# Three small reorderings in an attention-plus-MoE kernel: four products moved between transposes and x chunks, and an earlier place in the queue for a transposing DMA

## The chip, the cores and the metric

The kernel runs on one NeuronCore of a Trainium2 chip. The core has five engines that run their own instruction streams and wait for one another through semaphores: TensorE (PE, with its weight loads shown separately as PEld), VectorE (DVE), ScalarE (ACT), GpSimd (POOL) and SyncE (SP). SP computes nothing here; it issues DMAs, in order. The metric is the time of one execution on the device in microseconds (us), the median of several runs.

## What is computed

An "efficient attention" followed by a feed-forward layer with a snake activation. Eight batches of eight heads, 576 rows each, head dimension 64; the feed-forward part sees 4608 tokens of width 512 and a hidden width of 2048.

```python
q_s = softmax(q, axis=-1);  k_s = softmax(k, axis=2)
kv  = einsum('bhsd,bhse->bhde', k_s, v)
x   = einsum('bhsd,bhde->bhse', q_s, kv)          # then tokens x 512
h = x @ w_in
g = h + sin(alpha * h) ** 2 / alpha
out = g @ w_out
```

## The kernel before

**Tiles and stages.** The 4608 tokens are taken as nine tiles of 512 (`t` = 0 to 8). A tile needs the rows of one batch or of two neighbouring ones (576 rows against 512), so attention for batch `b` is worked off while tile `b - 1` is in its feed-forward part. The program order on every engine is written out by hand (`tc.manual_schedule()`), so an engine does exactly what the lines say, in their order; semaphores add only the waits.

**The feed-forward part of a tile.** `mm_h(t, ni)` makes one block of 128 hidden units: four matmuls of 512 columns from `win` and the transposed input `xT` into one PSUM bank (L254). ACT takes the sine (L260); the square is made by ACT (L262), POOL (L264) or DVE (L266); DVE combines both into `g` (L270), which also frees the bank. There are 16 blocks in a tile. The second products (`mm_o`, L274) multiply `g` with `wout`: 64 of them for a tile, 16 for each of four row blocks `j` of 128 rows. After a row block's sixteenth product, `evac_o` copies the bank into one of four buffers `o` (L286) and requests two stores on SP (L289). These products run one tile behind: a generator (`o_stream(t)`, or `o_quad` for tile 0) yields after each product, and `take(os, n)` takes the next `n`. So the kernel fills PE with products wherever something else would have to be waited for.

**Attention for a batch.** ACT takes the exponentials of q and k (L119), POOL or ACT and DVE cast v into `vb` (L138, L450). `norm_q` sums q's rows on DVE and divides (L146 to L153), giving `qn`. `kv_mm` makes kv on PE (L174, 72 small matmuls), `kv_norm` on DVE makes the block-diagonal `kbd` from it (L184, L187). x is `kbd` times the transposed q, `qT` (L223, L231), and a copy brings it to `xT` (L226, L468, L553, L558). `qT` comes about in two ways:

- Batches 0 and 1: by PE (`q_transpose_ii`, L203), into a PSUM bank and from there by a copy. For batch 1 this is `transpose_q1(ii)`, with a bank of pool `a` (two banks) and a copy on DVE (L458). `x_half(ii)`, the x matmuls of one half, takes its two banks from the same pool and is copied by ACT and DVE (L468).
- Batches 2 to 7: by a transposing DMA on SP (`q_transpose_dma`, L213). For batch 2 it is two DMAs, one for each half `ii`; chunks `c` = 0 and 1 of x need the first, chunks 2 and 3 the second. From batch 3 on it is one.

**Around the three places.** In tile 0's products (`o_quad`, L439 to L487) batch 1's attention is worked off: `x_half(0)`, `transpose_q1(1)`, two products, `kv_mm`, `kv_norm`, five products, `x_half(1)`. In tile 1's products (L534 to L560) batch 2's: 52 products are taken by L547, then come the four chunks of x with one product after each, and the last products after a further group of four x matmuls. In tiles 3 to 6 the loop at L592 runs over 16 blocks. At block `ni` = 4 it requests the transposing DMA for batch `t + 1` and, up to batch 7, the three loads of the batch after (`load_batch`, L98, 1.15 MB each). From block 9 on, `attn_back` (L569) uses the result, at every second block. After each block, `take` brings the number of products up to `want` (L602): 25, 27, 30, 32, 35 after blocks 0 to 4 in tile 3, and 23, 25, 28, 30, 33 in tiles 4 to 6.

SP's queue holds, in tile 3's first blocks: the stores of row block 0 of tile 2, the stores of its row block 1, the transposing DMA (which waits for POOL's `qn`), three loads.

Of the kernel before, what the change touches and what calls it, by code (L numbers as in the profile page):

```python
# [23 lines left out]
def kernel(  # L24
# [53 lines left out]
    def src_view(t, b):  # L78
        return t[b].rearrange("(i e) (p j) d -> (e p) i (j d)", e=2, j=J)
# [21 lines left out]
    def load_batch(b):  # L101
        load("q", q, b)
        load("k", k, b)
        load("v", v, b)
# [6 lines left out]
    def load_wout(n0, n1):  # L111
        nc.gpsimd.dma_start(out=wout[:, n0:n1, :], in_=wout_v[:, n0:n1, :])
# [13 lines left out]
    def exp_half(name, b, ii, j1=J):  # L126
        if ii == 0:
            A[name + "e", b] = att2.tile([128, J, 4 * D], BF16, name=name + "e")
        exp_to(A[name + "e", b][:, 0:j1], staged[name, b][:, :, 0:j1], (ii,))
# [60 lines left out]
    def q_tile(b):  # L190
        if ("qT", b) not in A:
            A["qT", b] = att2.tile([128, 2, J, 128], BF16, name="qT")
        return A["qT", b]
# [6 lines left out]
    def q_transpose_ii(b, ii, j0, j1, tp):  # L200

        for j in range(j0, j1):
            nc.tensor.transpose(tp[:, j - j0], A["qn", b][:, ii, j], identb)  # L203
# [36 lines left out]
    def bank(kind):  # L240

        if kind == "k":
            return ps_k.tile([128, 2, MF], F32, name="kvp", tag="a")[:, 0]
        pool = {"a": lambda: ps_h[0], "b": lambda: ps_h[1], "l": lambda: ps_l, "o": lambda: ps_o}[kind]()
        return pool.tile([128, MF], F32, name={"l": "lp", "o": "op"}.get(kind, "hp"), tag=kind)
# [140 lines left out]
    def h_slot(t, ni, sq, lag):  # L386
        hp = mm_h(t, ni, 2 if ni < (4, 1, 0)[min(t, 2)] else 0)
        lag.append((t, ni, hp, sine(t, ni, hp, sq)))

    def flush(lag, keep):  # L390
        while len(lag) > keep:
            combine(*lag.pop(0))

    def o_quad(t, accs, engs):

        R = range(4)
        by_m, by_n = [(n, m) for m in R for n in R], [(n, m) for n in R for m in R]
        orders = [by_m, by_n, by_n, by_n[:8] + [(n, m) for m in R for n in (2, 3)]]
        for c in R:
            for n, m in orders[c]:  # L400
                mm_o(t, m, 4 * c + n, accs[m])
                if c == 3 and n == 3:
                    evac_o(t, m, accs[m], engs[m])
                yield

    def take(it, n=1000):
        for _ in range(n):
            if next(it, 0) == 0:
                return
# [4 lines left out]
    with ES:  # L414
        def load_q1(ii):
            if ii == 0:
                staged["q", 1] = stage.tile([128, 4, J, D], F32, name="st_q", tag="st")
            st = staged["q", 1]
            DVE_CP(st[:, ii, 0, 0:1], zero)
            nc.sync.dma_start(out=st[:, ii::2, 0:8].rearrange("p i j d -> p i (j d)"),  # L420
                              in_=src_view(q, 1)[:, ii::2, 0:8 * D])

        def load_kv1():
            for n in "kv":
                staged[n, 1] = stage.tile([128, 4, J, D], F32, name=f"st_{n}", tag="st")
            for ii in range(2):
                for n, t in (("k", k), ("v", v)):
                    nc.sync.dma_start(out=staged[n, 1][:, ii::2].rearrange("p i j d -> p i (j d)"),
                                      in_=src_view(t, 1)[:, ii::2])

        late = {6: lambda: load_q1(0), 8: lambda: load_wout(8, 12), 10: lambda: load_wout(12, 14), 13: lambda: (load_q1(1), load_kv1())}
        for ni in range(nN):
            h_slot(0, ni, "DPPAPPAPPAAPPAPD"[ni], lag)
            flush(lag, 1)
            if ni in late:
                late[ni]()
        flush(lag, 0)

        accs = [bank(kind) for kind in "bbll"]  # L439
        os = o_quad(0, accs, [DVE_CP, ACT_CP, DVE_CP, DVE_CP])  # L440
        take(os, 46)
        for ii in range(2):
            exp_half("q", 1, ii, 8)
        norm_q(1, [GP, V], 8)
        GP_CP(held, staged["k", 1][:, 0, 0, 0:1])
        load_wout(14, 16)

        def cast_v1(ii, eng):
            vv = vb[1].rearrange("p j (i c) -> p i j c", i=4)
            eng(vv[:, 2 * ii:2 * ii + 2, :, 0:D], staged["v", 1][:, ii::2])  # L450

        exp_half("k", 1, 0)
        cast_v1(0, ACT_CP)
        exp_half("k", 1, 1)
        def transpose_q1(ii):
            tp = ps_h[0].tile([128, 8, 128], BF16, name="tp", tag="a")
            q_transpose_ii(1, ii, 0, 8, tp)
            DVE_CP(q_tile(1)[:, ii, 0:8], tp)  # L458

        transpose_q1(0)  # L460
        take(os, 4)

        def x_half(ii):
            xp = [bank("a") for _ in range(2)]
            for e in range(2):
                attn_chunk(1, 2 * ii + e, 0, 8, xp[e])
            for e in range(2):
                (ACT_CP, DVE_CP)[e](xT[:, 2 * ii + e, MF:2 * MF], xp[e])  # L468

        kv_mm(1, 0, ps_k, split=True)  # L470
        kv_norm(1, 0, 1)
        for b in range(2):
            DVE_CP(q8[:, 0, b, 0:1], zero)
            nc.sync.dma_start(out=q8[:, :, b], in_=src_view(q, b)[:, :, 8 * D:J * D])
        load_batch(2)
        cast_v1(1, DVE_CP)
        take(os, 4)
        x_half(0)
        transpose_q1(1)
        take(os, 2)  # L480
        kv_mm(1, 1, ps_k, split=True)
        kv_norm(1, 1, 2)
        take(os, 5)
        x_half(1)
        exp_to(A["qe", 1][:, J - 2:J], q8)
        nc.scalar.activation(zero, zero, AX.Sin)
        take(os)  # L487
        for ki in range(2):
            mm_h(1, 0, ki, ki + 1)
        norm_q8()  # L490
        load("q", q, 3)
        load("k", k, 3)
        load("v", v, 3)

        def late_q8(ni):
            if ni == 11:
                tp = ps_k.tile([128, 2, 2, 128], BF16, name="tp", tag="a")
                for b in range(2):
                    for ii in range(2):
                        nc.tensor.transpose(tp[:, ii, b], A["qe", 1][:, J - 2 + b, ii * 128:(ii + 1) * 128], identb)  # L500
                DVE_CP(A["qT", 1][:, :, J - 2:J], tp)
            elif ni == 15:
                xp = ps_k.tile([128, 4, 2, P], F32, name="xp", tag="a")
                for c in range(4):
                    ii, e = divmod(c, 2)
                    for b in range(2):
                        nc.tensor.matmul(xp[:, c, b], kbd[b][:, e, ii],
                                         A["qT", 1][:, ii, J - 2 + b, e * 64:(e + 1) * 64], start=True, stop=True)
                DVE_CP(xT[:, :, 16 * P:18 * P], xp.rearrange("p c b n -> p c (b n)"))

        for ni in range(nN):
            h_slot(1, ni, SQ[ni], lag)
            flush(lag, 1)
            late_q8(ni)
        cast_v(2, [GP_CP, GP_CP])
        flush(lag, 0)
# [17 lines left out]
    os = o_stream(1)  # L534
# [15 lines left out]
    for c in range(4):  # L550
        xp = bank("aabb"[c])[:, 0:6 * P]
        attn_chunk(2, c, 0, 6, xp)
        (ACT_CP, DVE_CP)[c % 2](xT[:, c, c0:c0 + 6 * P], xp)  # L553
        take(os, 1)
    xp = ps_a.tile([128, 2, 512], F32, name="xp", tag="a")[:, :, 0:6 * P]
    for c in range(4):
        attn_chunk(2, c, 6, 9, xp[:, c // 2, (c % 2) * 3 * P:(c % 2 + 1) * 3 * P])
# [22 lines left out]
    for t in range(3, nT):  # L580
        b = t + 1 if t + 1 < B else None
        os = o_stream(t - 1)
        done = 0
        if b is not None:

            exp_q(b)
            exp_k(b)
            cast_v(b, [GP_CP, GP_CP])
            norm_q(b, [GP])
            take(os, 8)  # L590
            done = 8
        for ni in range(nN):  # L592
            hp = mm_h(t, ni)
            if b is not None:
                if ni == 4:
                    q_transpose_dma(b)
                    if b + 1 < B:
                        load_batch(b + 1)
                attn_back(b, ni - 5)
            s = sine(t, ni, hp, "A")  # L600
            combine(t, ni, hp, s)
            want = 23 + 2 * (t == 3) + 21 * ni // 8 if b is not None else 4 * (ni + 1)  # L602
            take(os, min(64, want) - done)
            done = min(64, want)
        take(os)
# [36 lines left out]
```

## Time and profile before

| | |
|---|---|
| median of 3 runs | 284.15 us (284.1 to 284.52) |
| the profiled execution, whole time | 284.61 us |
| its span, first to last instruction | 282.8 us |
| granted TensorE clock | 1.00 throughout |
| busy time PE / ACT / DVE / POOL | 272.3 / 225.2 / 189.1 / 83.6 us |
| first product stretch (tile 0's, batch 1's attention) | about 28 to 45.6 us |
| second product stretch (tile 1's, batch 2's attention) | about 60 to 76 us |
| tiles 3 to 6 | from 93.5 us on, some 29.4 us each |

The rows of a timeline read: start, duration (us), engine, line, operation, output<-input, tile of the array, shape, count of merged instructions, and in brackets the engine's idle time before it with what ended it. A matmul's end is modelled, and the next one starts before it. "SPq" rows are the issue of a DMA, not its transfer; the chain of waits shows a transfer from its request to its landing. Releasers are inferred, and where several things were waited for the latest is named.

### The profile page before, as it was taken

Reading aid. Unit: us, or ns where it says so; the run is one execution under the profiler, and the core shown is the slowest. Engines: PE = TensorE matmul, PEld = TensorE weight load, DVE = VectorE, ACT = ScalarE, POOL = GpSimd, SP = SyncE. Lnnn points to the kernel's source line nnn. Section 1 sums busy time; section 2 is a strip of 40 time slices with the busy share of each in tenths; the row PEclk is TensorE's granted clock in tenths of the full one; section 3 lists DMA queues with packets and bytes.
Section 4 is the critical chain, followed back from the end, with each engine's and each line's share of the span. In section 5 each row is a group of like instructions: output and inputs, shape, how many; then the busy total and the mean of one; then the engine's idle time right before and its main releaser. Section 6 shows DMA issues by size and latency. Waiting matters only on the chain.

```text
span 282.8 us, 4841 instructions
## 1 busy us (share of the span) xinstructions
PE 272.3 (96%) x1857; PEld 128.0 (45%) x1857; DVE 189.1 (67%) x286; ACT 225.2 (80%) x320; POOL 83.6 (30%) x80
## 2 busy tenths in 40 slices
PE   2999999999999999999999999999999999999994
PEld 1444444444444444444544444444444444444443
DVE  3968778899977768756875677667775555555412
ACT  4889667999489998899989998999877777777400
POOL 2989411777666550035012500241000000000000
PEclk9999999999999999999999999999999999999999
DMA  6999989996599018931991099019011111111143
GB/s 256 306 195 234 300 278 320 361 352 226 125 233 387 6 37 198 386 116 35 263 398 42 14 271 404 23 24 160 2 37 37 37 39 37 37 37 43 44 103 74
DMA packets 39127, 45.80 MB, mean 162 GB/s; under 512 B 17072, under 2 KB 22464, under 8 KB 39104
## 3 DMA queue, kind: packets, MB, share of 16 engines
q1 hardware_dynamic: 33360, 40.57, 47.0%
q0 software_dynamic: 5552, 4.79, 10.1%
q8 instruction: 14, 0.23, 0.3%
q10 hardware_dynamic: 192, 0.14, 0.2%
q14 instruction: 9, 0.07, 0.1%
HBM read 36.71 MB, written 9.44 MB: 163 GB/s over the span
## 4 chain that ended last, share of the span: by engine, by line
PE 82%; DMA 6%; ACT 5%; issue 2%; DVE 2%; POOL 1%; SPq 1%
PE hp L254 35%; PE op L274 32%; PE lp L274 2%; PE hp L274 2%; PE lp L254 2%; DMA qT<-qn 2%; ACT s L260 2%; DMA win<-in_moe_w_in_dram 2%; PE xp L223 2%; DMA st_k<-in_k_dram 2%; PE kvp L174 1%; PE op L612 1%; PE op L254 1%; PE kvp L254 1%; DVE qs L151 1%
## 5 line engine op out<-in xcount | busy, mean ns | idle before, releaser
L270 DVE SCALAR_TENSOR_TENSOR g<-s,inva_sb,hp 128x512 bf16<-128x512 f32 x128 | 94.3, 746 | 58.6 <-ACT s L262 52.9
L254 PE MATMUL hp<-xT,win 128*128 128x512 bf16 x512 | 128.3, 379 | 0.7 <-DMA win<-in_moe_w_in_dram 0.7
L274 PE MATMUL op<-wout,g 128*128 128x512 bf16 x496 | 124.1, 379 | 0.0
L260 ACT ACTIVATE s<-hp,alpha_sb 128x512 f32<-128x512 f32 x128 | 86.2, 682 | 24.3 <-PE hp L254 23.9
L254 PEld LDWEIGHTS <-win 128*128 128x128 bf16 x576 | 56.0, 98 | 67.9 <-DMA win<-in_moe_w_in_dram 0.8
L274 PEld LDWEIGHTS <-g 128*128 128x128 bf16 x560 | 53.9, 98 | 61.1 <-issue 0.4
L262 ACT ACTIVATE s<-s 128x512 f32<-128x512 f32 x112 | 70.5, 630 | 3.5
L264 POOL TENSOR_TENSOR s<-s 128x512 f32<-128x512 f32 x29 | 30.3, 1061 | 21.6 <-ACT s L260 21.6
L153 POOL TENSOR_TENSOR qn<-qe,qs 128x1152 bf16<-128x1152 bf16 (+1 forms) x12 | 25.1, 2110 | 33.0 <-DVE qs L147 24.3
L286 DVE COPY o<-op 128x512 f32<-128x512 f32 (+2 forms) x33 | 22.1, 670 | 9.9 <-PE op L274 7.6
L138 POOL CAST vb<-st_v 128x1152 bf16<-128x1152 f32 x12 | 14.7, 1257 | 46.9 <-DMA st_v<-in_v_dram 32.9
L119 ACT ACTIVATE qe<-st_q 128x1152 bf16<-128x1152 f32 (+1 forms) x16 | 17.5, 1130 | 5.0 <-DMA st_q<-in_q_dram 4.8
L119 ACT ACTIVATE ke<-st_k 128x1152 bf16<-128x1152 f32 x16 | 17.9, 1151 | 1.5 <-DMA st_k<-in_k_dram 1.5
L146 DVE TENSOR_REDUCE qs<-qe 128x36 f32<-128x2304 bf16 x5 | 12.8, 2553 | 7.9 <-ACT qe L119 7.9
L226 DVE CAST xT<-xp 128x512 bf16<-128x512 f32 (+1 forms) x18 | 13.5, 751 | 0.1
L151 DVE TENSOR_REDUCE qs<-qe 128x16 f32<-128x1024 bf16 (+1 forms) x6 | 7.5, 1252 | 3.8 <-ACT qe L119 3.8
L119 ACT ACT_TABLE_LOAD x7 | 9.0, 1283 | 1.3 <-PEq L626 1.2
L274 PE MATMUL lp<-wout,g 128*128 128x512 bf16 x32 | 9.1, 380 | 0.0
L274 PE MATMUL hp<-wout,g 128*128 128x512 bf16 x32 | 8.9, 380 | 0.0
L223 PE MATMUL xp<-qT,kbd 128*128 128x256 bf16 (+1 forms) x40 | 8.2, 286 | 0.3 <-DMA qT<-qn 0.3
L174 PEld LDWEIGHTS <-ke 64*64 64x64 bf16 x576 | 5.7, 108 | 4.7 <-ACT vb L329 1.3
L187 DVE TENSOR_TENSOR kbd<-kvp,kvr 64x256 bf16<-64x256 f32 (+1 forms) x20 | 7.4, 368 | 0.5
(83 smaller groups left out, 135.6 us busy)
## 6 DMA issues: line engine op xcount, KB each, us to landing
out_dram<-o SPq DMA_DIRECT2D x70, 128.0 KB, 2.4
st_q<-in_q_dram SPq DMA_DIRECT2D x6, 1152.0 KB, 6.3
st_k<-in_k_dram SPq DMA_DIRECT2D x6, 1152.0 KB, 8.8
st_v<-in_v_dram SPq DMA_DIRECT2D x6, 1152.0 KB, 11.1
st_k<-in_k_dram SPq DMA_DIRECT2D x4, 576.0 KB, 6.7
st_q<-in_q_dram SPq DMA_DIRECT2D x4, 512.0 KB, 5.2
st_v<-in_v_dram SPq DMA_DIRECT2D x3, 576.0 KB, 7.6
wout<-in_moe_w_out_dram POOLq DMA_DIRECT2D x3, 512.0 KB, 9.6
```

The lines of the kernel that those rows point to most:

```text
L119: nc.scalar.activation(dst[:, :, ii * 128:(ii + 1) * 128].rearrange("p j (x d) -> p x j d", x=2), src[:, ii::2], AX.Exp)
L138: engs[ii](vv[:, 2 * ii:2 * ii + 2, :, 0:D], staged["v", b][:, ii::2])
L153: engs[ii % len(engs)].tensor_tensor(qn[:, ii, 0:j1].rearrange("p j (x d) -> p j x d", x=2), qe[:, ii], part.unsqueeze(3).to_broadcast([12 ...
L223: nc.tensor.matmul(xp[:, e, 0:n], kt[:, e, ii], qT[:, ii, j0:j1, e * 64:(e + 1) * 64], start=True, stop=True)
L226: eng(xT[:, 2 * ii:2 * ii + 2, c0:c0 + n], xp[:, :, 0:n])
L254: nc.tensor.matmul(hp, win[:, ki, ni * 128:(ni + 1) * 128], xT[:, ki, t * MF % NX:t * MF % NX + MF], start=(ki == 0), stop=(ki == 3))
L260: nc.scalar.activation(s, hp, AX.Sin, scale=alpha_sb[:, ni:ni + 1])
L262: nc.scalar.activation(s, s, AX.Square)
L264: nc.gpsimd.tensor_tensor(s, s, s, op=ALU.mult)
L270: nc.vector.scalar_tensor_tensor(G[t][:, ni], in0=s, scalar=inva_sb[:, ni:ni + 1], in1=hp, op0=ALU.mult, op1=ALU.add)
L274: nc.tensor.matmul(acc, G[t][:, ni, j * 128:(j + 1) * 128], wout[:, ni, :], start=(ni == 0), stop=(ni == nN - 1))
L286: eng(o[:, cols], acc)
```

## The change

Two products move from after batch 1's second transposes to before them. Two products move from the group after batch 2's x chunks to the place between its second and third chunk. And in tiles 3 to 6 the transposing DMA of q, with the three loads that follow it, is requested at block 3 and not at block 4.

```diff
         x_half(0)
+        take(os, 2)
         transpose_q1(1)
-        take(os, 2)
         kv_mm(1, 1, ps_k, split=True)
...
         (ACT_CP, DVE_CP)[c % 2](xT[:, c, c0:c0 + 6 * P], xp)
-        take(os, 1)
+        take(os, 3 if c == 1 else 1)
...
             if b is not None:
-                if ni == 4:
+                if ni == 3:
                     q_transpose_dma(b)
                     if b + 1 < B:
                         load_batch(b + 1)
```

In the order of instructions, PE has the two products of batch 1 ahead of all eight transposes, and the two products of batch 2 ahead of chunk 2. DVE, ACT and POOL keep their order. SP's order changes in tile 3 alone: the transposing DMA and the three loads stand ahead of the two stores of row block 1 there. In tiles 4 to 6 no store lies between the two positions.

## The prediction

> **What bounds the kernel now.** I read the page's busy times and chain first, then the busy time by stretch, then the order of instructions around the places that the diff touches.
>
> ```profile
> PE 272.3 (96%) x1857; PEld 128.0 (45%) x1857; DVE 189.1 (67%) x286; ACT 225.2 (80%) x320; POOL 83.6 (30%) x80
> PE 82%; DMA 6%; ACT 5%; issue 2%; DVE 2%; POOL 1%; SPq 1%
> ```
>
> TensorE is the bound: 272.3 of 282.8 us busy. The chain gives DMA 6%, of which qT<-qn is 2.4% or 6.8 us. This isn't time to be won: the chain was followed back through these transfers (2.86 and 3.98 us), but PE worked during most of both. What can be won is PE's own pauses, so I asked for the stretches (columns: stretch, its length, then each engine's busy time with instructions):
>
> ```profile
> 28.00:45.60 17.60, 17.14 (x159) 8.13 (x158) 13.55 (x26) 10.16 (x13) 4.62 (x5) 1.00 0.99 277
> 60.00:76.00 16.00, 15.93 (x150) 7.57 (x147) 15.27 (x22) 13.36 (x15) 10.79 (x8) 1.00 0.72 233
> 94.00:112.00 18.00, 17.70 (x152) 8.17 (x151) 12.60 (x18) 17.51 (x25) 6.52 (x5) 1.00 0.33 70
> 112.00:141.00 29.00, 29.00 (x208) 13.69 (x206) 20.18 (x29) 26.64 (x39) 6.48 (x4) 1.00 0.68 204
> ```
>
> Only the first three hold a pause (0.46, 0.07 and 0.30 us; from 112 to 264 us there is none). These figures are too small, for a matmul shows about 0.38 us while the next one starts earlier: eight of 512 columns start within 1.73 us (74.23 to 75.96), so one costs 0.216 us of PE's stream. A true pause is start to start, less 0.216 per matmul between.
>
> **Place A, batch 1's second transposes.** PE's, PEld's and DVE's instructions around them:
>
> ```profile
> 40.96 0.61 PE L231 MATMUL hp<-qT,kbd 128*128 128x512 bf16 x2
> 42.02 0.61 PE L203 MATMUL tp<-identb,qn 128*128 128x128 bf16 x8 [0.46 <-ACT xT L468]
> ```
> ```profile
> 44.38 0.21 PEld L231 LDWEIGHTS <-kbd 128*128 128x128 bf16 x2 [0.22 <-DVE kbd L187]
> ```
> ```profile
> 41.48 0.77 DVE L450 CAST vb<-st_v 128x1152 bf16<-128x1152 f32 x1 [0.33 <-DMA st_v<-in_v_dram]
> 42.28 0.69 DVE L468 CAST xT<-hp 128x512 bf16<-128x512 f32 x1
> 42.89 0.68 DVE L458 COPY qT<-tp 128x1024 bf16<-128x1024 bf16 x1
> 43.54 0.17 DVE L184 RECIPROCAL kvr<-kvp 128x2 f32<-128x2 f32 x1
> 43.74 0.59 DVE L187 TENSOR_TENSOR kbd<-kvp,kvr 64x128 bf16<-64x128 f32 x2
> ```
>
> The two x matmuls occupy PE to 40.96 + 0.43 = 41.39; the transposes start at 42.02, since their bank is freed by ACT's copy (L468, 41.39 to 41.97). Pause: 0.63 us. The change puts two products there, 0.43 us, to 41.82. The transposes still start at 42.02 and take 0.45 us, to 42.47. Then kv follows without the two products: 0.09 us to change over (42.90 to 42.99 before), 0.42 us of matmuls, to 42.98; five products, 1.08 us, to 44.06. There x_half(1) needs kbd, and kbd is made by DVE, whose five rows follow one another without a gap from 41.48 on, the first having waited for st_v. None of them starts sooner: L458 waits for DVE, not for PE's transposes (done by about 42.64, against 42.89). So the weights still load at 44.38 and the x matmuls still start at 44.50, which is where PE stands now too (44.28 + 0.216). The pause moves from 42.0 to 44.1: 0.20 us stay and 0.44 us are new. I cost A at **0**. Upper bound: should st_v land 0.33 us sooner than in this execution, DVE's chain starts that much sooner and A gains 0.33. A loss is excluded as long as the transposes start at 42.02: ACT's copy sets that, and the copy hangs on the x matmul ahead of it.
>
> **Place B, batch 2's x chunks.** PE's instructions, and the chain at that time:
>
> ```profile
> 72.70 0.38 PE L274 MATMUL op<-wout,g 128*128 128x512 bf16 x1
> 73.15 0.32 PE L231 MATMUL hp<-qT,kbd 128*128 128x384 bf16 x1
> ```
> ```profile
> 70.25 2.86 DMA qT<-qn
> 73.11 0.04 issue
> ```
>
> The third chunk waits for the second transposing DMA, which lands at 73.11. Pause: 73.15 - (72.70 + 0.216) = 0.23 us. Two more products ahead of it bring the chunk to 72.53 + 0.16 + 3 x 0.216 = 73.34, after the landing: the pause is filled, with 0.19 us to spare. The two products are missing from the eight after the chunks, so tile 2's first block starts at 75.96 - 0.23 = 75.73. What it waits for: bank a (ACT's copy of chunk 0, done at 73.0) and chunks 1 to 3 in xT, needed by its second to fourth matmul. The last copy on DVE ends near 75.7 and the fourth matmul starts at 76.38: 0.7 us of cover. So B gains **0.23**. Bounds 0 and 0.23 (nothing more is idle there).
>
> In the Trainium skill, "TensorE: Matmul & The Clock Gate", section "Back-to-back issue gap", matmuls of 512 columns in a real stream are given about 131 ns each. By that figure two products would fill only 0.26 us of A's pause, and B's would just be covered; the 0.216 us of this trace decides.
>
> Is B's gain kept until place C? After 76 us ACT waits for PE at 77.02 and 83.05 (3.04 and 0.64 us idle), so the sines follow PE; POOL's first square (78.49) is held by norm_q and doesn't move, but its block's bank is wanted only at 81.97, against a combine done at 80.3. Tightest is tile 3's block 4: it starts at 102.13, its bank is free at 102.0. That combine follows ACT, which runs without idle time from 83.05, where it followed PE; both move by 0.23.
>
> **Place C, tile 3's q.** PE, SP's queue, and POOL:
>
> ```profile
> 110.31 1.03 PE L254 MATMUL hp<-xT,win 128*128 128x512 bf16 x4
> 111.63 0.39 PE L223 MATMUL xp<-qT,kbd 128*128 128x256 bf16 x2 [0.30 <-DMA qT<-qn]
> ```
> ```profile
> 102.68 4.82 SPq L289 DMA_DIRECT2D out_dram<-o  x4
> 107.60 1.87 SPq L213 DMA_TRANSPOSE qT<-qn  x1
> ```
> ```profile
> 99.64 4.21 POOL L153 TENSOR_TENSOR qn<-qe,qs 128x1152 bf16<-128x1152 bf16 x2 [3.33 <-issue]
> ```
>
> Pause: 111.63 - (110.31 + 4 x 0.216) = 0.46 us; tile 4 goes from the same block to its x matmuls in 0.86 us (139.80 to 140.66), with none. The request is queued on SP behind the two stores of tile 2's second row block, whose copy (DVE, 105.69) comes late, while qn was ready at 99.64 + 4.21 = 103.85. At block 3 the request stands ahead of these stores: block 3's share of products is the one that ends at number 32 and evacuates. The first two stores are issued by 103.8, so the request goes out at about 103.87 and lands, at the same 3.98 us, by 107.9; PE wants it at 111.17, less B's 0.23. Cover: 3.1 us. C gains **0.46**, bounds 0 and 0.46.
>
> What else moves with it: the three loads of batch 5 go out 3.7 us sooner, and the two stores behind them, at about 107.5 instead of 106.39. The stores now lie behind 3.4 MB: stores that do took up to 10.4 us to land. Their buffer (one of four) is written again four copies later, near 136 us (136.27). Nobody waits.
>
> In tiles 4 to 6 no store lies between the two positions (30 products are done by block 3's end, 33 by block 4's), SP's order is the same, and its request starts as soon as POOL ends: 133.32 against 129.08 + 4.22 = 133.30, and the like at 162.41 and 191.83. Block 3 or 4 means nothing to a queue that waits for POOL: **0**.
>
> **Sum.** 0 + 0.23 + 0.46 = 0.69 us. The profiled execution took 284.61 (a span of 282.8, and 1.8 around it), 0.46 above the median of the three shown, 284.15. It should come to 283.92, and the median to 284.15 - 0.69 = **283.46**.
>
> **Rivals.**
> 1. *The time comes back as another wait (283.7 to 284.15).* A pause on PE that is filled helps only if no other wait is as late. For: A is such a case, and ACT is busy 17.51 of 18 us between 94 and 112. Against: after C ACT waits for PE again (0.64 us at 113.36, 0.38 at 119.68), and the banks have the margins named above. Losing C alone gives 284.15 - 0.23 = 283.92, losing B alone 283.69, losing both 284.15. In this rival stands too that half of the change (A, tiles 4 to 6) does nothing, which my sum holds already.
> 2. *A pays as well (283.13).* 283.46 - 0.33, if st_v lands sooner than in this execution. Against: it is a fixed queue of loads from the same start.
> 3. *Slower: GpSimd's cast of v beside DVE (285.2).* The loads of batch 5 land 3.7 us sooner, so POOL's cast of v (L138, 122.38, which waited for them) runs at about 118.5, beside DVE's copies and combines of tile 3's blocks 13 to 15. For: DVE's product at 67.54, beside POOL, took 1.97 us for 1152 columns where 1024 took 1.23, 0.59 more than in proportion; three operations stretched so cost 1.8 us: 283.46 + 1.8 = 285.2. Against: beside that same cast, DVE's combine at 122.46 took 0.74 and its copy at 123.11 0.68, as elsewhere, and DVE waits 0.98 us for ACT at 121.06. It decides once 0.69 + 0.57 = 1.26 us of it reach PE.
>
> The Trainium skill, "GPSIMD Engine Reference", section "Specifications", says that GpSimd shares its path to SBUF with VectorE, with contention for some DVE instructions, those with two SBUF inputs among them; a combine reads one input from PSUM, so it would leave the third rival without a price.
>
> **How the numbers follow.** A measurement of this kernel tells about 0.2%, 0.57 us, from no change. Forecast 0.61, rival 1 0.23, rival 2 0.07, rival 3 0.09. The forecast's own range is 283.3 to 283.7 (the three runs before spread over 0.42). Faster by over 0.2% means below 283.58: 0.85 of the forecast and all of rival 2, 0.59; the rest of the forecast and rival 1 are within 0.2%, 0.32; slower 0.09. The range goes from rival 2 (283.1) to nearly all of rival 1 (284.1), and leaves out rival 3 and the edges.
>
> **What would show it.** A: the transposes still at 42.02, a new pause of some 0.4 us ahead of the x matmuls at 44.5 and tile 1's first block still at 45.58. B: no wait for qT between the second and third chunk, tile 2's first block at 75.7. C: SP's request at about 103.6, ahead of two stores, and no wait for qT at L223; all later PE rows 0.69 us sooner. I am wrong if the x matmuls of A start before 44.4, if a wait for ACT or a bank appears on PE in tiles 2 to 4, or if the last matmul isn't some 0.7 us sooner.

## The result, and the profile after

| | before | after |
|---|---|---|
| median, 17 runs each, one beside the other | 284.52 us (lowest 283.97) | 283.37 us (lowest 282.98) |
| ratio of the undisturbed runs, 95% interval | | 0.9957 (0.9944 to 0.9970) |
| the profiled execution: whole, span | 284.61, 282.8 us | 283.31, 281.5 us |

The change makes the kernel 0.43% faster (0.30 to 0.56%), some 1.2 us (0.85 to 1.6). The time of 283.37 lies close to the 283.46 that was forecast, but the gain is larger than the sum of 0.69 us: beside the new kernel, the old one measured 284.52 and not 284.15. So the closeness is in part luck: the starting value was 0.37 us too low and the gain 0.46 us too small, and the two nearly cancel. The larger gain is what has to be explained. One run of the kernel before, 288.73 us, 1.7% above its fastest, counts as disturbed.

The page of the kernel after, busy times and chain:

```profile
PE 270.0 (96%) x1828; PEld 128.3 (46%) x1857; DVE 188.8 (67%) x286; ACT 225.3 (80%) x320; POOL 83.5 (30%) x80
PE 85%; DMA 7%; POOL 2%; DVE 2%; issue 1%; ACT 1%; SPq 1%; ACTq 0%
```
PE's count is 29 matmuls lower than before while its weight loads are as many: records are missing, so the lower busy time tells nothing. The time has to be read from start to start. These are the same landmarks in each trace: the first product of the first stretch, the x matmuls of `x_half(0)` and `x_half(1)`, tile 1's first block, and so on to the first matmul of the last row block (L612).

| from one landmark to the next, us | before | after | difference |
|---|---|---|---|
| start of the span to the first product | 28.23 | 27.80 | -0.43 |
| first product to `x_half(0)` | 12.73 | 12.86 | +0.13 |
| `x_half(0)` to `x_half(1)`: place A | 3.54 | 3.34 | -0.20 |
| to tile 1's first block | 1.08 | 1.09 | +0.01 |
| to the first x chunk of batch 2 | 26.58 | 26.52 | -0.06 |
| to tile 2's first block: place B | 3.80 | 3.57 | -0.23 |
| to tile 3's block 9 | 34.35 | 34.35 | 0 |
| block 9 to tile 3's x matmuls: place C | 1.32 | 0.86 | -0.46 |
| from there to L612 | 163.96 | 163.95 | -0.01 |

The rows add up to -1.25 us, from 275.59 to 274.34 at L612 (the table's figures are rounded). B and C gave what was forecast. A gave 0.20, and 0.05 behind it (0.01 lost and 0.06 gained), where nothing was forecast. What stands ahead of `x_half(0)`, the first 41 us, which the change doesn't touch, gave 0.30 in this pair of executions.

Place A after the change, PE, then PE's weight loads, then DVE:

```profile
41.10 0.59 PE L274 MATMUL lp<-wout,g 128*128 128x512 bf16 x2
41.72 0.61 PE L203 MATMUL tp<-identb,qn 128*128 128x128 bf16 x8
42.26 0.48 PE L174 MATMUL kvp<-vb,ke 64*64 64x65 bf16 x36
...
43.54 0.38 PE L274 MATMUL lp<-wout,g 128*128 128x512 bf16 x1
44.00 0.60 PE L231 MATMUL hp<-qT,kbd 128*128 128x512 bf16 x2
```
```profile
43.99 0.11 PEld L231 LDWEIGHTS <-kbd 128*128 128x128 bf16 x2 [0.57 <-DVE kbd L187]
```
```profile
41.16 0.76 DVE L450 CAST vb<-st_v 128x1152 bf16<-128x1152 f32 x1 [0.31 <-DMA st_v<-in_v_dram]
41.95 0.69 DVE L468 CAST xT<-hp 128x512 bf16<-128x512 f32 x1
42.56 0.68 DVE L458 COPY qT<-tp 128x1024 bf16<-128x1024 bf16 x1
43.16 0.16 DVE L184 RECIPROCAL kvr<-kvp 128x2 f32<-128x2 f32 x1
43.35 0.59 DVE L187 TENSOR_TENSOR kbd<-kvp,kvr 64x128 bf16<-64x128 f32 x2
```

The two products now fill most of the old pause (41.10 to 41.53, transposes at 41.72), and a new pause stands ahead of the x matmuls: 44.00 - (43.54 + 0.216) = 0.24 us, with the weight load waiting for kbd. That is the picture of the forecast. What differs is the end: the x matmul starts at 44.00, 0.01 us after its weights begin to load, not 0.12 after. The load costs PE's stream next to nothing here: tile 1's first block follows the x matmul by 1.09 us, against 1.08 before.

Place C after the change, SP's queue and PE:

```profile
101.91 1.12 SPq L289 DMA_DIRECT2D out_dram<-o  x2
103.13 1.95 SPq L213 DMA_TRANSPOSE qT<-qn  x1
...
106.96 1.33 SPq L289 DMA_DIRECT2D out_dram<-o  x2
```
```profile
109.53 1.02 PE L254 MATMUL hp<-xT,win 128*128 128x512 bf16 x4
110.39 0.38 PE L223 MATMUL xp<-qT,kbd 128*128 128x256 bf16 x2
```

The request stands ahead of the two stores, 4.5 us sooner in the span (107.60 before), and the x matmuls follow block 9 after its four matmuls (4 x 0.216 = 0.86), without a wait.

### The profile page after: what moved, and what is told of

Read it like the earlier page. It is cut to its first block, busy times and chain, and to the rows that moved or that the text cites. A ratio compares the mean times of both kernels' runs of the same rounds, so it can differ in the third digit from the quotient of the medians.

```text
span 281.5 us, 4812 instructions
## 1 busy us (share of the span) xinstructions
PE 270.0 (96%) x1828; PEld 128.3 (46%) x1857; DVE 188.8 (67%) x286; ACT 225.3 (80%) x320; POOL 83.5 (30%) x80
## 4 chain that ended last, share of the span: by engine, by line
PE 85%; DMA 7%; POOL 2%; DVE 2%; issue 1%; ACT 1%; SPq 1%; ACTq 0%
PE op L274 38%; PE hp L254 37%; DMA st_v<-in_v_dram 4%; PE xp L223 2%; DMA win<-in_moe_w_in_dram 2%; DMA st_k<-in_k_dram 2%; PE kvp L174 2%; PE lp L254 2%; POOL s L264 1%; PE op L612 1%; PE op L254 1%; ACT s L260 1%; PE kvp L254 1%; POOL st_v L299 1%; DVE g L270 1%
## 5 line engine op out<-in xcount | busy, mean ns | idle before, releaser
L274 PE MATMUL op<-wout,g 128*128 128x512 bf16 x477 | 121.6, 379 | 1.4 <-issue 0.6
```

Of the source, the lines that this page charges most:

```text
L274: nc.tensor.matmul(acc, G[t][:, ni, j * 128:(j + 1) * 128], wout[:, ni, :], start=(ni == 0), stop=(ni == nN - 1))
```

## The experiments

Four kernels came first, each timed beside the kernel before on one chip (12 runs each, 35 of before, whose median was 284.43 us).

**A alone.**

```diff
         x_half(0)
+        take(os, 2)
         transpose_q1(1)
-        take(os, 2)
```

> Only the two products ahead of batch 1's second transposes (place A). The prediction's theory: A is worth 0, within 0.1 us of before; in the trace the transposes wait for ACT's copy as before, and a pause of about 0.4 us stands ahead of the x matmuls that need kbd. Rival theory, that A is where the 0.3 to 0.5 us come from by which the whole change gained more than the 0.69 us of the sum: 0.3 to 0.5 us faster, and tile 1's first block starts that much sooner after the stretch's first product. Third theory, that the surplus comes from the first 28 us and not from the change: no difference here.

Measured: 284.08 us, ratio 0.9984 (0.9961 to 1.0007). The comparison alone doesn't settle it; the trace does. `x_half(0)` to `x_half(1)` is 3.23 us against 3.54: 0.31 us. The prediction's 0 falls, and the rival's size (0.3 to 0.5) is met at this place. By the landmark that the expectation names, from the stretch's first product to tile 1's first block, it is only 0.21 us (17.14 against 17.35), for the part ahead of `x_half(0)`, which the edit doesn't touch, took 0.10 longer in this execution.

**B alone.**

```diff
-        take(os, 1)
+        take(os, 3 if c == 1 else 1)
```

> Only the two products between batch 2's second and third x chunk (place B). The prediction's theory: 0.23 us faster, no wait for qT ahead of the third chunk, tile 2's first block 0.23 us sooner after the first chunk; place C's wait for qT stays at 0.46. Rival: the pause comes back as a wait for a copy or for ACT in tile 2, then 0. The third theory adds nothing to the difference.

Measured: 284.38 us, ratio 0.9993 (0.9974 to 1.0011). In its trace the third chunk doesn't wait, and tile 2's first block comes 3.57 us after the first chunk, as forecast. But so it does in two kernels that don't have B at all, see below.

**C alone.**

```diff
-                if ni == 4:
+                if ni == 3:
                     q_transpose_dma(b)
```

> Only the earlier request of the transposing DMA in tiles 3 to 6 (place C). The prediction's theory: 0.46 us faster, all of it in tile 3, whose x matmuls follow block 9 without a pause. Rival: the earlier loads or the later stores cost part of it, then 0 to 0.3 us. If C alone gives 0.8 us or more, the surplus over the sum lies here, against the prediction's bound.

Measured: 284.06 us, ratio 0.9977 (0.9959 to 0.9995), 0.37 us by the medians. In the trace block 9 is followed by the x matmuls after 0.87 us; the pause of 0.46 is gone and nothing takes its place: from the x matmuls to L612 it is 163.95 us, as before.

**C in tiles 4 to 6 alone.**

```diff
-                if ni == 4:
+                if ni == (4 if t == 3 else 3):
                     q_transpose_dma(b)
```

> The earlier request in tiles 4 to 6 alone, and in tile 3 at block 4 as before. Every engine's order of instructions is that of before, so the prediction's theory says 0.00 us, and the measured difference shows what the comparison itself can tell. The theory that the surplus lies in how a newly built program happens to start says that this one, too, is some 0.3 to 0.5 us away from before.

Measured: 284.30 us, ratio 0.9992 (0.9973 to 1.0011). As forecast, nothing; with each engine's order unchanged this kernel is another execution of the kernel before. As such it showed that B's pause isn't always there. PE's instructions at the chunks, and SP's first transposing DMA, in this kernel:

```profile
72.09 0.33 PE L231 MATMUL hp<-qT,kbd 128*128 128x384 bf16 x1
72.25 0.38 PE L274 MATMUL op<-wout,g 128*128 128x512 bf16 x1
72.47 0.33 PE L231 MATMUL hp<-qT,kbd 128*128 128x384 bf16 x1
```
```profile
67.87 1.38 SPq L213 DMA_TRANSPOSE qT<-qn  x1
```

The third chunk follows the product after 72.47 - 72.25 = 0.22 us: no pause. SP took 1.38 us to issue the first of the two DMAs, against 1.82 us in the profile of before, and the second is issued only after it.

Then four kernels on a second chip (12 runs each, 35 of before, median 284.39): whether A pays in the whole, and what limits it.

**B and C without A** (the diffs above), and **the whole change again.**

> The change without its first part: B and C, A as before. The prediction's theory (A is worth 0): 0.69 us faster than before, and the same as the whole change run beside it. The theory formed after the first four runs (A is worth 0.2 to 0.35 us, B 0.05 to 0.23 by execution, C 0.46): about 0.55 us faster than before, and 0.2 to 0.35 us slower than the whole change.

> The whole change again, for the comparison with the other three on the same chip. The prediction's theory: 0.69 us faster than before. The later theory: 0.8 to 1.0 us faster.

Measured: B and C 283.72 us, 0.9976 (0.9955 to 0.9997); the whole 283.49 us, 0.9968 (0.9949 to 0.9988). By the medians 0.67 and 0.90 us: A is worth 0.23 in this comparison, whose intervals overlap. By the traces `x_half(0)` to `x_half(1)` takes 3.53 us without A and 3.21 with it, 0.32.

**The whole change with the copy of the transposes on ACT, and the kernel before with that copy alone.** The edit, in both:

```diff
             q_transpose_ii(1, ii, 0, 8, tp)
-            DVE_CP(q_tile(1)[:, ii, 0:8], tp)
+            (DVE_CP, ACT_CP)[ii](q_tile(1)[:, ii, 0:8], tp)
```

> The whole change, and the copy of batch 1's second transposes (L458) on ACT, which is idle for 2 us there, and not on DVE. The later theory says that after the change the x matmuls of x_half(1) wait for kbd at the end of a chain on DVE (cast of v, copy of x, copy of the transposes, kv_norm), so that taking 0.6 us out of that chain removes the pause ahead of them: kbd some 0.4 us sooner, the x matmuls 0.2 to 0.4 us sooner against the first product of the stretch, the kernel 0.2 to 0.4 us faster than the whole change. Rival, that PE's own products set the start of the x matmuls: no difference to the whole change.

> The kernel before with that copy on ACT alone. If the pause of A is on PE as the prediction says (five products end just when kbd is ready), a sooner kbd finds PE still at its products, and the kernel is within 0.1 us of before: the two edits pay only together. If DVE's chain were the limit in the kernel before as well, this alone would give 0.2 to 0.4 us.

Measured: the whole with it 283.30 us, 0.9969 (0.9946 to 0.9993); before with it 284.52 us, 1.001 (0.9984 to 1.0035). Both profiles are of executions that began late (the first product at 29.49 and 29.35 us, PE waiting 0.79 and 0.87 us for batch 0's cast of v), so only the distances behind it are used. With the whole change `x_half(0)` to `x_half(1)` is 3.10 us: exactly the two products less than 3.53, no pause ahead of `x_half(1)` left. In the kernel before it is 3.53 as ever. That kernel doesn't test what it was meant to, for kbd came no sooner: DVE's L184 waits 0.88 us there for kv on PE, and kbd is ready 3.37 us after `x_half(0)`, as in the profile of before. What set the x matmuls is read from the starts instead: in every execution without A's edit, and in those with the copy on ACT, they start 0.216 us after the last product, without a pause. So the limits are these: before the change, PE's own five products; after it, DVE's chain to kbd; with the copy on ACT, PE again.

Last, **the whole change and its ACT variant side by side** on a third chip (6 runs each, 11 of before, median 284.67), and **the kernel before in two more executions.**

> The whole change beside its variant with the copy of the transposes on ACT, on one chip. The later theory (A 0.25 to 0.38, B 0 to 0.24 by execution, C 0.46): 0.8 to 1.0 us faster than before. The prediction's sum: 0.69.

> The whole change with the copy of batch 1's second transposes on ACT. If the pause ahead of x_half(1) that the change leaves (0.1 to 0.2 us in the traces) is all that goes, it is 0.1 to 0.2 us faster than the whole change, and the x matmuls of x_half(1) follow those of x_half(0) by 3.10 us, against 3.2 to 3.3 in the whole change. Rival: the longer copy on ACT delays something in tile 1, then it is the same as the whole change.

> The kernel before, one more execution, to see which of its pauses are there each time. The prediction took all from one execution: 0.63 us ahead of the second transposes, 0.23 ahead of the third chunk, 0.46 at tile 3's qT. The later theory: the first and the last are there every time, the one ahead of the third chunk only where the first transposing DMA takes 1.8 us to issue and not 1.4; and the stretch's first product starts anywhere from 27.8 to 28.3 us.

> The kernel before once more, another execution, with what was expected of the first look: the pause ahead of the third chunk goes with the issue time of the first transposing DMA, the other two are there each time.

Measured: the whole 283.23 us, 0.9959 (0.9945 to 0.9973); the variant 283.30 us, 0.9956 (0.9941 to 0.9972). The variant's trace shows what was expected, PE's weights and DVE:

```profile
44.49 0.21 PEld L231 LDWEIGHTS <-kbd 128*128 128x128 bf16 x2 [0.22 <-DVE kbd L187]
```
```profile
43.64 0.17 DVE L184 RECIPROCAL kvr<-kvp 128x2 f32<-128x2 f32 x1 [0.55 <-PE kvp L174]
```

DVE now waits 0.55 us for kv, the copy being gone from its queue, and the x matmuls come 3.10 us after those of `x_half(0)`, at 44.60, where PE's products end. Against 3.2 to 3.3 in the whole change that is 0.1 to 0.2 us, and 0.05 of it is given back in tile 1. On the clock the variant came out 0.19 us ahead in one comparison and 0.07 behind in the other: no difference is shown, and there is no version that is shown to beat the change.

The two executions of before took 284.71 and 284.78 us, first product at 28.13 and 28.40. Their pauses at A and C were there (3.54 and 3.53 us; 0.48 and 0.49 us). At B one had none, and the other this, PE's chunks and SP's first transposing DMA:

```profile
72.59 0.38 PE L274 MATMUL op<-wout,g 128*128 128x512 bf16 x1
73.25 0.32 PE L231 MATMUL hp<-qT,kbd 128*128 128x384 bf16 x1 [0.28 <-DMA qT<-qn]
```
```profile
68.22 2.04 SPq L213 DMA_TRANSPOSE qT<-qn  x1
```

The pause is 73.25 - (72.59 + 0.216) = 0.44 us, twice that of the first profile. Over the seven executions that don't have B's edit:

| issue of the first transposing DMA, us | 1.38 | 1.39 | 1.57 | 1.62 | 1.80 | 1.82 | 2.04 |
|---|---|---|---|---|---|---|---|
| pause ahead of the third chunk, us | 0 | 0 | 0 | 0.02 | 0.20 | 0.23 | 0.44 |

(The kernels: C in tiles 4 to 6, A alone, the second of these two executions, before with the ACT copy, C alone, the profile of before, the first of the two. The 1.39 is worked out: the pair took 2.78 and the second of it 1.29, with 0.10 between.) Above 1.6 us the pause is the issue time less 1.6. Why SP needs longer for the same DMA in one execution than in another wasn't tried and stays open.

## Why the prediction was right, and where it wasn't

**What bounds the kernel, and where time could come from: right.** PE's pauses, read start to start, were the whole gain that the traces show behind `x_half(0)`. The rest of PE's stream kept its length in every trace: from tile 2's first block to tile 3's block 9 34.34 to 34.35 us, from tile 3's x matmuls to L612 163.94 to 163.96 us. Rival 1 (the time comes back as another wait) is thereby out, but for A, where the forecast itself had the new pause, and where it is smaller than forecast.

**C: right in place and size.** 0.46 us forecast; the pause was 0.46 to 0.54 in the seven traces without C's edit in tile 3, and 0.00 or 0.01 in the seven with it. The request came at 103.13; forecast was 103.6 less the 0.43 by which this execution began sooner. The stores that it passed went out at 106.96, and no one waited. Tiles 4 to 6: nothing, as forecast.

**B: right for the execution it was read from, wrong as a bound.** "Bounds 0 and 0.23 (nothing more is idle there)" took one execution for all. The pause was 0 to 0.44 us in seven, 0.13 on average; the two products, 0.43 us, cover nearly all of it. In the profile after, the gain was 0.23.

**A: the step that failed.** The prediction put it so: "So the weights still load at 44.38 and the x matmuls still start at 44.50, which is where PE stands now too", and therefore A at 0. The traces show 0.20, 0.31, 0.32 and 0.26 us in the four kernels with A (3.34, 3.23, 3.21 and 3.28 us against 3.53 or 3.54), and a further 0.05 in tile 1 up to the x matmuls of late q rows (14.11 or 14.12 us against 14.16 or 14.17; why this part shortens wasn't looked into). The prediction had also named a sign of being wrong, x matmuls of A that start before 44.4. They start at 44.00, or at 44.30 if `x_half(0)` is laid where it was before (40.96), so by its own sign this part is wrong; and the pause it expected ahead of them, some 0.4 us, is 0.24. The picture was right, the pause did move to the x matmuls, but the chain was over-long in two places:

- The weight load was counted in series, 0.12 us between 44.38 and 44.50. Before the change, the x matmul began at 44.50 because PE's products ended there; the load had merely happened in the meantime. Where PE stands idle, the matmul begins with the load: 43.99 and 44.00 after the change. The profile of before shows the same at C, where the load (the row below) and the matmul both start at 111.63. The Trainium skill says so too ("TensorE: Matmul & The Clock Gate", section "Architectural detail: the array is 16× 32×32, not 1× 128×128": a matmul can begin before its weights are completely loaded); I didn't hold it against this step.

```profile
111.63 0.11 PEld L223 LDWEIGHTS <-kbd 128*128 128x128 bf16 x2 [0.79 <-DMA qT<-qn]
```

- "None of them starts sooner" was true of that execution alone, and there not quite. In the six other executions without A's edit that have the copy on DVE (the kernel before twice more, B alone, C alone, C in tiles 4 to 6, B and C), DVE's L184 waits 0.17 or 0.18 us for kv on PE, which stands behind the two products that the change moves ahead; the row below is of the second further execution of before. In the first profile st_v had come 0.33 us late, and that wait was hidden but for 0.05 (L458 to L184 took 0.65 us before, 0.60 after).

```profile
43.94 0.17 DVE L184 RECIPROCAL kvr<-kvp 128x2 f32<-128x2 f32 x1 [0.17 <-PE kvp L174]
```

In the pair of profiles the load starts 3.42 us after `x_half(0)` before and 3.33 after (0.09), and the x matmul 0.12 and 0.01 us after the load (0.11): together 0.20. In the other kernels with A it is more, where DVE's cast of v (L450), which waits for st_v, starts sooner. Times from `x_half(0)`:

| kernel with A | change | A alone | the whole again | the whole, third chip |
|---|---|---|---|---|
| cast of v starts, us | 0.50 | 0.38 | 0.37 | 0.44 |
| x matmuls of `x_half(1)`, us | 3.34 | 3.23 | 3.21 | 3.28 |

The second row is the first plus 2.84 or 2.85 each time: DVE's chain from the cast on sets it. Without A's edit the cast starts anywhere from 0.17 to 0.52 us, and the x matmuls stay at 3.53 or 3.54. So rival 2 was right that A pays and that st_v decides how much, but the size of its bound, 0.33, was met by luck: it was to take st_v 0.33 us sooner, and 0.15 was enough. Nor is it a bound: by the same relation a cast that starts 0.26 us or less after `x_half(0)`, as in three of the executions without the edit, would leave PE's products as the limit, 3.10 us and a gain of 0.43. That is an estimate; no run with the copy on DVE shows it. And "a fixed queue of loads from the same start" doesn't land at a fixed time.

**The sum.** With the means of the traces A is 0.27 + 0.05, B 0.13, C 0.49: 0.94 us, inside the intervals of the first comparison (0.85 to 1.6) and the third (0.8 to 1.6), both of which leave out the forecast's 0.69, and near the second's medians (0.90), whose interval holds both. The first and third comparisons gave 1.15 and 1.44 us by the medians. What lies above 0.94 isn't settled. In eleven of the fourteen profiles the first product starts between 27.79 and 28.40, with and without the change (the kernel before at 28.13 to 28.40, in the order of before also at 27.79; the whole at 27.80 to 28.19), so the first pair's 0.43 there isn't shown to be a gain of the change; whether the medians hold some of this wasn't separated.

**Rival 3: out.** POOL's cast did move up, to 118.60, beside DVE's combines. POOL, then DVE, of the kernel after:

```profile
118.60 2.26 POOL L138 CAST vb<-st_v 128x1152 bf16<-128x1152 f32 x2 [15.53 <-DMA st_v<-in_v_dram]
```
```profile
119.81 0.75 DVE L270 SCALAR_TENSOR_TENSOR g<-s,inva_sb,hp 128x512 bf16<-128x512 f32 x1 [0.98 <-ACT s L262]
120.47 0.82 DVE L226 CAST xT<-xp 128x640 bf16<-128x640 f32 x1
```

0.75 and 0.82 us, as at the same place before (121.06 and 121.72): no price.

## What to carry to other kernels

Where one engine is busy 96% of the time, list its pauses start to start and price each edit by the pause that it fills and by the next chain that comes due; a pause is worth filling only as far as the second-latest chain allows. When two chains end within some 0.1 us of each other in one profile, don't take the tie for a wall: ask for each link whether it was waiting or merely happened in time, and look at a second execution. A request that waits in an ordered queue behind work that comes late is moved ahead of that work, not just earlier in the program: where the order in the queue stayed, as in tiles 4 to 6, nothing came of it.

## What the runs showed of the hardware that wasn't expected

SP took from 1.38 to 2.04 us to issue the same transposing DMA (nine blocks of 128 columns) at the same place in different executions, and PE's wait for the next one followed it. And the start, the same instructions each time, put the first product at 27.79 to 28.40 us, or at 28.77 to 29.49 in the three profiles with the copy on ACT, in two of which PE waited 0.79 and 0.87 us for batch 0's cast of v on DVE. These three executions took longer than most of their kernels' runs (285.21, 286.19 and 283.99 us, medians 283.30, 284.52 and 283.30), and the medians lie within 0.2 us of those of the same kernels without the copy on ACT. So a late start isn't what that copy does to every execution; its cause stays open. Both spreads are as large as the gains that were looked for.
